# An adaptive-norm block with a long convolution and a shifted MLP on one core: second stage of one transform in groups of three, separate room for one modulation vector, and a new hand-written order

## The chip, the cores and the metric

The kernel runs on one core of one Trainium2 chip. The metric is the device time in microseconds, the median of several executions. Traces come from the hardware profiler and describe one execution each; the clock they name is the TensorE clock that the chip granted, as a share of full speed.

## What is computed

The sequence has S=2048 positions of D=640 channels, and the MLP is F=1728 wide. All inputs are bfloat16. Cut to what matters:

```python
def reference(A_q, A_k, A_v, A_shift_k, A_ssm_k, A_ssm_D, B_x, B_w1, B_w2, B_w3, B_w4, c, w_mod):
    def A(q, k, v, shift_k, ssm_k, ssm_D):
        k_shift = sum over t of k delayed by 3-t, times shift_k[:, 3-t]      # 4 taps
        kv = k_shift * v
        y = irfft(rfft(kv, 2S) * rfft(ssm_k, 2S))[:S]                        # causal, along S
        return q * (y + kv * ssm_D)
    def B(x, w1, w2, w3, w4):
        h = gelu(layernorm(x) @ w1)
        # four quarters of the channels, shifted along S by +1, -1, +2, -2
        x1 = x + concat(shifted quarters of h) @ w2
        return x1 + gelu(layernorm(x1) @ w3) @ w4
    x = A_q
    sa, ca, ga, sb, cb, gb = split(silu(c) @ w_mod, 6)
    h = layernorm(x) * (1 + ca) + sa
    x = x + ga * A(h, A_k, A_v, A_shift_k, A_ssm_k, A_ssm_D)
    h = layernorm(x) * (1 + cb) + sb
    return x + gb * B(h, B_w1, B_w2, B_w3, B_w4)
```

## The kernel before

**The convolution as matmuls.** The transform of length 4096 is done in two stages of 64. The filter ssm_k (called s) and the product kv pass through the same steps. DVE transposes in 32x32 blocks bring the data into slots (`to_slots`, L395). Stage one multiplies by a small constant matrix F1bd (matmuls L408) and writes its result into T01, whose halves T0 and T1 hold 320 of the 640 channels each. Stage two multiplies by the twiddled matrices Gs, kept in tile RG, one for each of 32 values of k. For s, `stage2` (L416 to L432) takes one k at a time over all channels: four matmuls of 64x320 (L425) and one evacuation of 640 elements per partition into KSX, tile R3. For kv, `stage2_half` (L434 to L452) takes three values of k at a time over one half of the channels: twelve matmuls of 64x160 (L446) and one evacuation of 960 elements into XS, tile R5. Every evacuation of PSUM goes through `evac`, whose work lies on ACT (L208) or on DVE (L210), as the order says. Between the two passes `k_shift` (L472 to L489) forms kv from the transposed k and v.

**Inverse stage one** (`inverse1`, L622 to L649) runs ten steps i=0 to 9, five for each half. A step needs KSX also with its two partition halves swapped. Two DMAs make that copy into one of four ring buffers KSY (in RG, RK, RK and Rb), one issued by SP and one by POOL:

```python
for o in range(2):
    dma("SP" if o == 0 else "POOL", 256, lambda q, o=o: q.dma_start(ky[64 * o:64 * o + 64, :], kx[64 - 64 * o:128 - 64 * o, :]), r=[kxk], w=[kk + ("y",)], rate=222.0)
```

DVE then forms two products TA and TB (L632), PE sums them with two constant matrices (L643, L644), and two evacuations write back into T01. **Inverse stage two** (`inverse2`, L664, matmuls L676) reads all of T01 and leaves y for one to three of the 16 sequence tiles at a time. The constants Hs it uses lie in RH, brought there by sixteen small copies at L591.

**The modulation vectors.** `mod_half` (L501 to L527) loads 400 KB of w_mod for half a vector (L503), multiplies by silu(c) (L509) and copies the result into modv. Halves 0 to 5 (sa, ca, ga) come early. Halves 6 to 11 (cb, sb, gb) have their weights in R3, columns 0 to 9600, which KSX occupies until the products have read it.

**Layer norms and the MLP.** ln1, for the first norm, has its statistics on DVE or ACT and a small end (`ln1_fin`, L572 to L577) on POOL. `make_q` (L616, L617) applies sa, ca, ga. `chain_a`, `chain_b` and `chain_c` (L747 to L804) form x after A, then h, then the normed h, with squares summed on ACT at L744 and the small end of the norm at L711 to L734; the first transposes go through PE, later ones through DMA (L780). `mm_w1` (L833, L843, gelu L835 and L849), `mm_w2` (L888, L895), `mm_w3` (L922, gelu L926) and `mm_w4` (L952, L943) follow, and L975 to L984 finish a tile: times gb, plus x, and store. `last_tile` (L986) does that in halves for the last. w1 and w2 go into RG (L1007 to L1010). w3 goes into T0 in one transfer and w4 into T1 in one large and two small ones (L1022 to L1025), once `inverse2` has read T01. x is loaded by `x_load` (L540) twice: into Ra for tiles 0 to 7, and later for tiles 8 to 15 in four pieces of 160 KB for each group of four tiles, called cg0 to cg3.

**What sets the order.** Every step is a task with a number, its engine, its costs and the pieces of tiles that it reads and writes. The string ORDER lists all tasks in the order in which they are issued, with a letter for the engine and the places in PSUM. SP, POOL, DVE, ACT and PE each work through their own part of it strictly in order, and wait where data demand it. So an instruction that waits holds everything behind it on its engine, and a transfer issued by POOL waits for POOL's arithmetic ahead of it.

Of the kernel before, what the change touches and what calls it, by code (L numbers as in the profile page):

```python
# [12 lines left out]
ALU = mybir.AluOpType  # L13
PSUM = bass.MemoryType.PSUM

S, D, F = 2048, 640, 1728
P = 128
NT = S // P
ND = D // P
NF = (F + P - 1) // P  # L20
# [6 lines left out]
18D 19G 20D 50G 21G 23D 22D 25A 27G 29D 30A 36G 37G 24A 28D 31A 2S 0S 68G 4S 26G 69D 90P:0 91A 6S 84P:1 85A 3S 72G 86P:2 87A 5S 32D 73D 102P:3 38G  # L27
104P:0 103A 8S 70G 71D 39G 40A 106P:1 107A 49G 41G 98P:2 88P:3 89A 99A 105D 118P:0 9S 74D 94P:1 75D 95A 112P:3 110P:2 119D 52D 1S 66D 67D 10S 108P:0
111A 113A 109A 42G 11S 43G 44A 33G 116P:1 117D 45D 114P:2 82P:3 54A 96P:0 122P:1 34G 47S 46G 51D 97A 7S 115A 53A 92P:0 35S 201S 48S 12S 93A 83D 76P:3
77A 100P:2 123D 14S 203S 204S 78P:1 101D 80P:0 202S 56G 136D 13S 120P:3 219S 79A 81A 179P:2 55G 180A 193P:1 194A 15S 16S 121D 195P:0 196D 199P:2  # L30
145P:3 200A 147P:1 146D 57G 148A 185P:0 175P:2 176A 186D 141P:3 142D 58G 139P:1 140A 17S 216S 165P:0 166A 177P:2 178D 163P:3 164A 149P:1 150D 59G
189P:0 190A 167P:2 168D 187P:3 188A 143P:1 144D 161P:0 162A 171P:2 172A 181P:3 182D 169P:1 157P:0 65G 158D 170A 159P:2 160A 151P:3 152D 155P:1 153P:0
156A 154D 191P:2 192A 183P:3 184D 173P:1 174A 137P:0 138A 258P:2 250D 197P:3 198A 259A 207D 256P:1 257A 60A 208D 126P:0 127D 264P:3 265A 210A 124P:2
125D 260P:1 261A 61G 251D 62G 266P:3 267A 130P:0 131D 63G 64A 222S 128P:2 129D 252D 205A 220P:1 221A 206D 209G 268P:3 269A 228S 262P:0 263A 272P:1
254P:2 255A 338S 132P:3 133D 134P:0 135D 253D 273A 211A 278P:2 279A 284P:1 270P:3 339G 217P:0 437D 225S 274P:2 285A 223P:1 218A 224D 231S 282P:0 283D
271A 275A 288P:3 289A 280P:1 281D 286P:2 443D 287A 290P:0 229P:3 248S 245G 230D 291A 292P:1 362S 293A 440D 294P:2 295D 304P:3 226P:0 227D 244G 305A
298P:1 306P:2 308P:0 299A 232P:3 446D 309A 276P:1 277A 249G 247S 307D 233D 444D 300P:2 310P:0 311A 246G 301D 312P:3 313D 296P:1 297A 336P:2 337A
302P:0 303D 314P:3 315A 239S 332P:1 333A 238S 237G 328P:2 234G 334P:0 335A 329A 441D 326P:3 327A 341D 322P:1 330P:0 331A 243S 242S 235G 340D 342P:2
343A 344P:3 345A 323D 320P:1 321A 316P:0 317A 241S 240G 236S 346S 348D 347G 349D 350P:2 351A 352P:3 318P:1 319A 356D 354S 355G 357D 358P:0 359A 363G
360P:2 361A 324P:1 325A 370S 364D 365D 368P:0 366P:2 371G 353A 372D 378S 373D 379G 369A 381D 380D 376P:1 374P:3 388D 367A 375A 387G 377A 384P:0 385A  # L40
382P:2 383A 386S 395G 389D 392P:3 390P:1 212G 394S 397D 396D 213A 400P:0 402S 391A 404D 403G 405D 401A 398P:2 399A 393A 421S 422P:1 406P:0 412D 407A
410S 411G 413D 408P:2 418S 445D 416P:3 414P:0 415A 409D 417D 419P:2 420D 436G 442D 452P:30 447D 214A 423D 427S 428P:2 453A 438D 429A 454D 424S 425P:1
426A 430S 431P:3 449A 432A 439D 448D 503D 504D 505A 489P:02 544D 524D 545D 215G 433S 450D 434P:1 537A 525D 435A 547D 456S 526A 527D 455S 546A 557A
490A 467S 506G 507G 482P:31 508D 509D 510A 538D 528G 548G 464S 484A 485G 549D 529D 483A 495P:01 550D 551A 451D 497A 486P:31 530D 531A 469S 511G 512G
462S 496A 491A 487A 463S 532D 533G 552D 553G 459S 461G 466S 572D 573D 574A 465S 575D 576D 577A 488A 513D 514P:0 534D 535P:2 458S 554D 555P:3 515D
521P:0 522A 578D 579G 584A 536D 556D 473D 580D 468S 460S 581D 542P:2 543A 582D 583A 492P:31 494A 540P:0 585D 586D 587A 562P:2 457S 563A 539D 588D
560P:1 519P:2 516D 517D 638D 639D 541A 589G 561A 590A 518D 635D 593D 594P:0 591P:1 520A 564P:2 636D 640A 474D 595D 592D 604P:0 498S 641G 637A 493A
565D 566A 605A 642G 643D 647D 502G 602P:1 603A 567D 568G 475G 648D 558D 649D 650A 569D 570P:3 644D 645D 646A 606P:2 500S 609P:0 571D 620P:1 651D 652G
624P:3 470D 655D 477A 656S 471A 653D 654S 621A 559D 622P:1 657A 625A 665P:3 610D 703D 607D 608A 479D 476D 472G 599D 663P:0 611A 612D 613G 626P:2 704D
623A 666A 614D 615P:1 664A 627A 617D 480A 618P:3 619D 616A 600D 601D 769D 658D 670P:0 671D 667P:2 668D 672A 770D 687P:3 688A 669A 681P:1 596D 501S  # L50
682A 673D 674G 675D 678A 499S 685P:0 676P:2 679P:3 705A 597D 598D 706D 707D 771A 677D 709G 686A 628P:1 629D 708A 683P:2 680A 753P:0 684A 749P:3 710G
715D 747P:1 716D 659D 772D 773D 754A 481G 774A 775D 478G 750A 689P:20 751P:3 794D 711D 712D 713D 776G 690P 777A 714A 717D 781A 782D 719G 718A 748A
720G 721A 722S 783D 784A 778D 791D 779D 780A 785D 786G 789A 630D 631S 723D 724S 725A 733P:1 660D 734A 691D 731P:2 790S 795D 661D 787D 788S 797P:1 634S
732A 735P:2 798A 697D 698D 662D 835D 799P:0 836D 692D 726D 727D 838D 695S 839D 752A 837A 840A 694S 800A 841G 842G 736D 738P:1 739D 741D 755P:32 801P:1
756P 843D 737A 740A 742G 844D 804P:0 743A 792D 845D 846A 847D 848D 849D 744S 850A 802D 803A 745D 702S 746S 819P:1 796D 728D 763D 813P:2 814A 633S 757D
632S 729D 851G 852G 815P:3 853D 730D 895D 854S 820A 855D 856S 859P:2 805D 806A 857P:0 817P:1 896D 793D 860A 758D 761S 807D 700S 808G 811D 809D 693S
858A 861P:2 862D 696S 897A 760S 764D 863A 812S 810S 898D 899D 879P:0 880A 955D 864P:2 900A 865D 818A 866A 767S 875P:0 873P:2 901G 816A 874A 877P:1
821P:32 956D 867D 868G 878A 876A 881P:10 869D 870S 871A 872S 822P 823D 902G 903A 904D 905D 958G 957A 959G 960A 961D 962D 963A 906A 964D 965G 907D 908D
909D 701S 699S 824D 827S 883D 939P:3 940A 910A 933P:1 882P 934A 966D 765S 967S 970P:3 971A 762S 937P:1 938A 911D 912G 915D 913D 914S 916S 919P:3 829D
920A 917P:2 968P:1 826S 918A 768S 969A 921P:3 922D 923A 828S 924P:2 973P:1 523G 925D 766S 884D 935P:3 974D 926A 759S 830D 972G 1007P:2 1008D 976P:1  # L60
977D 927G 979D 832S 1046D 936A 941P:32 943D 1010D 928G 931A 932S 831S 929A 930S 991P:1 885S 975A 889D 825S 890D 891S 978A 980G 942P 886S 987P:3 893S
988A 1009A 888S 989P:0 990A 985P:3 986A 949D 992A 1011G 981D 982S 983D 984S 1020P:2 1021A 1016P:0 1017A 1018P:3 1014P:1 1015A 834S 1019A 993P:20 833S
944D 948S 894S 1012D 1013S 1042P:1 1038P:3 887S 950D 951S 1047D 994P 946S 1043A 953S 995D 1036P:2 954S 1001D 947S 945S 1002D 1022P:10 892S 996D 1000S
997S 952S 1039A 1005S 1006S 1003S 1040P:3 1024D 1004S 1023P 999S 1025D 1028S 1030D 1041A 1027S 1029S 1026S 998S 1031D 1032S 1035S 1033S 1037A 1044P:13
1048D 1049D 1045P 1050S 1053S 1051S 1052S 1054D 1055D 1057A 1058S 1056S 1059A 1034S
# [72 lines left out]
def kernel(  # L138
# [277 lines left out]
    def stage2(XSd, dreg):  # L416
        for k in range(32):
            ps = Slot()

            def f(e, ps=ps, k=k):  # L420
                psv = pst(ps, name="ps_s2")[:, :, 0:320].rearrange("p g (h s) -> p g h s", h=2)
                for cc in range(2):
                    for g in range(2):
                        p = slice(64 * g, 64 * g + 64)
                        nc.tensor.matmul(psv[:, g], lhsT=Gs[p, k, 64 - 64 * cc:192 - 64 * cc], rhs=T1b[p, cc * 32 + k],  # L425
                                         start=(cc == 0), stop=(cc == 1), tile_position=(64 * g, 0))
            t0 = add("PE", 0.275, f, r=[("T01", 0, 20480), ("RG", 192 * k, 192 * k + 192)], alloc=ps, ni=8)
            w = [(dreg, 0, 20480, "s2")]
            if dreg == "R5":
                w += [("kT", 0, 5, "s2"), ("vT", 0, 5, "s2"), ("kTp", 0, 1, "s2")]  # L430
            t1 = evac(XSd[:, :, k, :], lambda t: t[:, :, 0:320].rearrange("p g x -> p x g"), 640, ps, w)
            dep(t1, t0)  # L432

    def stage2_half(h):  # L434
        for k0 in range(0, 32, 3):
            kn = min(3, 32 - k0)
            ps = Slot()

            def f(e, ps=ps, k0=k0, kn=kn, hh=h + 2):
# [159 lines left out]
    for h in range(2):  # L599
        stage2_half(h)  # L600
# [490 lines left out]
```

## Time and profile before

| | |
|---|---|
| runs | 314.98, 316.16, 315.33 us |
| median | 315.33 us |
| profiled execution | 314.98 us, of which the span of the profile is 313.0 us |
| PE, DVE, ACT, POOL busy | 270.4, 219.6, 208.5, 114.2 us |
| DMA moved | 35.75 MB |
| largest groups | L922 64.5 us, L952 59.2 us on PE |

A share of the whole span is a mean over stages that have different limits. The view of slices shows which engine is full at what time; the view of windows gives the busy time of each engine in a stretch; the view of waits says which instruction waited for what; and the chain that ended last follows the end of the kernel back from releaser to releaser. A row of the timeline gives the start, the length, the engine, the line and the tiles (`out<-in`) of one or several like instructions, and in brackets how long the engine stood idle before it and for whom.

### The profile page before, as it was taken

How to read it: one execution, taken by the hardware profiler on the slowest of the kernel's cores; microseconds unless marked ns; L12 is line 12 of the kernel's file. 1: busy time of each engine (PE TensorE's matmuls, PEld its weight loads, DVE VectorE, ACT ScalarE, POOL GpSimd, SP SyncE). 2: the span in 40 equal slices, each digit the busy share in tenths (PEclk: the TensorE clock that was granted, in tenths of full speed). 3: DMA queues.
4: the chain of work that ended last, by engine and by line, in shares of the span. 5: the costliest groups of instructions: out<-in, count | busy, mean ns of one | idle time of the engine just before them, and what ended most of it. 6: DMA issues, size and time to landing. Idle time of an engine off the chain costs nothing.

```text
span 313.0 us, 7669 instructions
## 1 busy us (share of the span) xinstructions
PE 270.4 (86%) x3050; PEld 206.3 (66%) x3054; DVE 219.6 (70%) x446; ACT 208.5 (67%) x351; POOL 114.2 (36%) x240
## 2 busy tenths in 40 slices
PE   0998999999973846687999978989999999999993
PEld 0655655787863624566788756678867887887771
DVE  8998999999964999989776586881627144511332
ACT  4888999999991789998974666625763445252110
POOL 4959333252663377255217520411423132010000
PEclk9999999999995965999999999999999999999998
DMA  6998999988999910521800031043021403131021
GB/s 187 260 220 163 225 205 223 232 217 212 225 276 269 211 37 3 197 100 26 282 24 0 2 68 38 8 94 70 5 54 32 76 0 65 42 70 37 2 71 42
DMA packets 58179, 35.75 MB, mean 114 GB/s; under 512 B 39936, under 2 KB 54912, under 8 KB 58144
## 3 DMA queue, kind: packets, MB, share of 16 engines
q1 hardware_dynamic: 56848, 31.49, 43.2%
q0 software_dynamic: 1200, 3.74, 5.1%
q8 instruction: 24, 0.39, 0.5%
q14 instruction: 11, 0.09, 0.1%
q10 hardware_dynamic: 96, 0.04, 0.1%
HBM read 16.31 MB, written 2.62 MB: 60 GB/s over the span
## 4 chain that ended last, share of the span: by engine, by line
PE 41%; DVE 12%; ACT 6%; DMA 5%; POOL 4%; issue 3%; SPq 0%; ACTq 0%; DVEq 0%; POOLq 0%
PE ps_w L952 15%; PE ps_w L922 14%; PE ps_w L888 5%; PE ps_w L833 3%; ACT RG L744 3%; DMA RG<-R 2%; DVE R L771 2%; DMA R<-RH 1%; DVE Ra L755 1%; POOL lnv L730 1%; PE ps_w1x L843 1%; PE ps_w L943 1%; DVE R L770 1%; PE ps_i L644 1%; DMA R<-RK 1%
## 5 line engine op out<-in xcount | busy, mean ns | idle before, releaser
L922 PE MATMUL ps_w<-R,T 128*128 128x256 bf16 (+1 forms) x630 | 64.5, 261 | 2.3 <-DVE RK L609 1.0
L922 PEld LDWEIGHTS <-T 128*128 128x128 bf16 x630 | 55.6, 98 | 10.2 <-issue 4.0
L926 ACT ACTIVATE R<-ps_w 128x1024 bf16<-128x1024 f32 (+2 forms) x36 | 29.3, 828 | 46.7 <-PE ps_w L922 46.7
L952 PE MATMUL ps_w<-T,R 128*128 128x320 bf16 x416 | 59.2, 299 | 0.0
L952 PEld LDWEIGHTS <-R 128*128 128x128 bf16 x416 | 40.3, 98 | 15.6 <-issue 0.5
L208 ACT CAST T<-ps_s 128x1024 bf16<-128x1024 f32 x35 | 33.3, 1027 | 4.1 <-PE ps_s L408 4.1
L975 DVE TENSOR_TENSOR T<-ps_w,R 128x640 bf16<-128x640 f32 x15 | 12.2, 821 | 29.0 <-PE ps_w L943 18.3
L408 PE MATMUL ps_s<-F1bd,Rb 128*128 128x256 bf16 x160 | 23.0, 294 | 9.4 <-DVE Rb L395 8.6
L744 ACT ACTIVATE RG<-R 128x640 bf16<-128x640 bf16 x32 | 23.4, 733 | 9.0 <-DVE R L895 6.4
L208 ACT CAST R<-ps_s 128x640 bf16<-128x640 f32 (+1 forms) x35 | 26.6, 843 | 0.8 <-PE ps_s L425 0.7
L408 PEld LDWEIGHTS <-Rb 128*128 128x128 bf16 x160 | 16.5, 105 | 15.4 <-DVE Rb L395 8.8
L644 PE MATMUL ps_i<-EB,Rb 128*128 128x128 bf16 x160 | 20.3, 227 | 6.7 <-DVE Rb L632 6.7
L895 DVE SCALAR_TENSOR_TENSOR R<-ps_w,R 128x640 bf16<-128x640 f32 x16 | 13.1, 821 | 18.5 <-PE ps_w L888 17.9
L730 POOL TENSOR_TENSOR lnv<-lnv,mhalf 128x2 f32<-128x2 f32 (+1 forms) x29 | 23.1, 796 | 2.3
L888 PE MATMUL ps_w<-RG,R 128*128 128x320 bf16 x160 | 23.6, 299 | 0.0
L208 ACT CAST T<-ps_i 128x1024 bf16<-128x1024 f32 x18 | 17.6, 1126 | 8.9 <-PE ps_i L644 8.9
L729 POOL TENSOR_TENSOR lnv<-stat,lnv 128x2 f32<-128x2 f32 x19 | 5.8, 306 | 46.0 <-ACT RG L744 31.6
L833 PE MATMUL ps_w<-R,RG 128*128 128x256 bf16 (+1 forms) x200 | 19.0, 251 | 3.2 <-ACT Rb L208 1.4
L643 PE MATMUL ps_i<-EA,Rb 128*128 128x128 bf16 x160 | 20.5, 227 | 1.4 <-DVE Rb L632 1.1
L644 PEld LDWEIGHTS <-Rb 128*128 128x128 bf16 x160 | 16.3, 103 | 7.4 <-DVE Rb L632 7.4
L833 PEld LDWEIGHTS <-RG 128*128 128x128 bf16 x200 | 16.4, 98 | 5.1 <-issue 2.4
L888 PEld LDWEIGHTS <-R 128*128 128x128 bf16 x160 | 15.4, 98 | 5.9 <-issue 0.3
(178 smaller groups left out, 528.5 us busy)
## 6 DMA issues: line engine op xcount, KB each, us to landing
Ra<-in_A_ssm_k_dram SPq DMA_DIRECT2D x5, 512.0 KB, 6.0
R<-in_w_mod_dram SPq DMA_DIRECT2D x6, 400.0 KB, 8.4
out_dram<-RH SPq DMA_DIRECT2D x60, 40.0 KB, 1.6
T<-in_B_w_dram SPq DMA_DIRECT2D x1, 2160.0 KB, 8.9
T<-in_B_w_dram SPq DMA_DIRECT2D x1, 2080.0 KB, 9.4
RH<-in_w_mod_dram SPq DMA_DIRECT2D x4, 400.0 KB, 4.6
Ra<-in_A_q_dram SPq DMA_DIRECT2D x4, 320.0 KB, 5.2
RK<-R POOLq DMA_DIRECT2D x5, 256.0 KB, 6.5
```

What stands on the lines that cost most here:

```text
L208: nc.scalar.copy(dst, src(ps.tile))
L408: nc.tensor.matmul(psv[:, ml, :], lhsT=xL[:, s0:s0 + P], rhs=F1r, start=True, stop=True)
L643: nc.tensor.matmul(psv[:, w, :], lhsT=Av[:, r_, :, g_], rhs=EAf, start=True, stop=False)
L644: nc.tensor.matmul(psv[:, w, :], lhsT=Bv[:, r_, :, g_], rhs=EBf, start=False, stop=True)
L730: nc.gpsimd.tensor_tensor(rs, rs, mhalf[:, 0:n], ALU.pow)
L744: add("ACT", 0.74, lambda e: nc.scalar.activation(junk, src, ACT.Square, scale=float(D) ** -0.5, accum_out=stat[:, li, 1, t:t + 1]), r=[sk ...
L833: nc.tensor.matmul(pt[:, fb, 0:cw], lhsT=w1_sb[:, b, 160 * fb:160 * fb + P], rhs=hT[:, b, 0:cw], start=(b == 0), stop=(b == ND - 1))
L888: nc.tensor.matmul(pt[:, hf, 0:320], lhsT=gsf[:, fb, c0:c0 + P], rhs=w2_sb[:, fb, 320 * hf:320 * hf + 320], start=(fb == 0), stop=(fb == 4))
L895: t1 = add("DVE", 0.82, lambda e, ps=ps, hv=hv, ix=ix: nc.vector.scalar_tensor_tensor(hv, ps.tile[:, :, 0:320], 1.0, hv, ALU.mult, ALU.add ...
L922: nc.tensor.matmul(pt[:, fl, 0:cw], lhsT=w3_sb[:, b, fb * P:(fb + 1) * P], rhs=xT[:, b, 0:cw], start=(b == 0), stop=(b == ND - 1))
L926: nc.scalar.activation(g3[g % 2][:, f0:f0 + fn, 0:cw], ps.tile[:, 0:fn, 0:cw], ACT.Gelu_apprx_tanh)
L952: nc.tensor.matmul(bank(i, hf), lhsT=gg[:, fb, i * P:(i + 1) * P], rhs=w4_sb[:, fb, 320 * hf:320 * hf + 320], start=(fb == 0 and i == 0), ...
```

## The change

Second stage of s: `stage2` is gone, and s goes through `stage2_half` as kv does, half by half. Of 32 evacuations of 640 elements 22 remain, twenty of 960 and two of 640; of 128 matmuls 64x320 there are 256 of 64x160. A group of the first half needs only the first half of T01.

Weights of modulation halves 10 and 11 (gb) go to R5, columns 13824 to 17024, in place of R3; the readers of cb and sb now depend on halves 6 to 9 alone.

w3 is loaded in five transfers of 128 rows and the main part of w4 in three, beside the two small ones as before.

The order is new throughout. What it moves:

- On POOL, `ln1_fin` of tiles 4 to 6 stands ahead of all the copies of `inverse1` but the first, and there is no arithmetic of POOL between copies i=1 and i=9.
- The copies of Gs (L354, L355) are all on SP, where three were on POOL. Two groups of angle operations (L307) go from POOL to DVE, and one at L349 from DVE to POOL.
- SP issues all loads of s before any transpose of k and v, the loads of x(0:8) earlier, and modulation halves 0 to 5 after all transposes.
- SP's queue at the end of `inverse1` is: half 7, copies i=8 and i=9, halves 9, 6, 11, 8, a piece of w2, half 10, w1, then pieces of x(8:16) among pieces of w2, then w3 in five with three of the pieces of x or w2 among them, w4's first small piece, x, two transposes, w4's second small piece and w4 in three (rows 8 to 13 first).
- `inverse2` takes its tiles in other groups: 0 to 2, then 14 and 15 with 3 and 4, 8 to 10, 5 to 7, and so on, and tiles 11 to 13 last, behind the w1 matmuls of the first tiles.

```diff
-    def stage2(XSd, dreg):
-        for k in range(32):
...
-                        nc.tensor.matmul(psv[:, g], lhsT=Gs[p, k, 64 - 64 * cc:192 - 64 * cc], rhs=T1b[p, cc * 32 + k],
-                                         start=(cc == 0), stop=(cc == 1), tile_position=(64 * g, 0))
...
-            t1 = evac(XSd[:, :, k, :], lambda t: t[:, :, 0:320].rearrange("p g x -> p x g"), 640, ps, w)
-    def stage2_half(h):
+    def stage2_half(XSd, dreg, h):
         for k0 in range(0, 32, 3):
             kn = min(3, 32 - k0)
...
-            w = [("R5", 10240 * h, 10240 * h + 10240, "s2"), ("kT", 4 * h, 5, "s2")] + ([("vT", 0, 5, "s2")] if h else [("kTp", 0, 1, "s2")])
-            t1 = evac(XS[:, 160 * h:160 * h + 160, k0:k0 + kn, :],
+            w = [(dreg, 10240 * h, 10240 * h + 10240, "s2")]
+            if dreg == "R5":
+                w += [("kT", 4 * h, 5, "s2")] + ([("vT", 0, 5, "s2")] if h else [("kTp", 0, 1, "s2")])
+            t1 = evac(XSd[:, 160 * h:160 * h + 160, k0:k0 + kn, :],
                       lambda t, kn=kn: t[:, :, 0:480].rearrange("p g (k s) -> p s k g", k=3)[:, :, 0:kn], 320 * kn, ps, w)
...
-    stage2(KSX, "R3")
+    for h in range(2):
+        stage2_half(KSX, "R3", h)
...
-    wl = [(R3[:, o:o + 1600].rearrange("p (b n) -> p b n", b=ND), ("R3", o, o + 1600)) for o in range(0, 9600, 1600)]
+    wl = [(R3[:, o:o + 1600].rearrange("p (b n) -> p b n", b=ND), ("R3", o, o + 1600)) for o in range(0, 6400, 1600)]
+    wl += [(R5[:, o:o + 1600].rearrange("p (b n) -> p b n", b=ND), ("R5", o, o + 1600)) for o in (13824, 15424)]
...
-    dma("SP", 2200, w3t[0], w=[("T01", 0, ND * FP)])
-    dma("SP", 2200, w3t[1], w=[("T01", 10240, 10240 + NF * D, "w4")])
+    for b in range(ND):
+        dma("SP", 440, lambda q, b=b: q.dma_start(w3_sb[:, b, 0:F], B_w3[b * P:(b + 1) * P, :]), w=[("T01", b * FP, b * FP + FP)])
+    for f0, f1 in ((0, 4), (4, 8), (8, NF - 1)):
+        dma("SP", 165 * (f1 - f0), lambda q, f0=f0, f1=f1: q.dma_start(w4_sb[:, f0:f1, :], B_w4[f0 * P:f1 * P, :].rearrange("(b p) n -> p b n", p=P)),
+            w=[("T01", 10240 + D * f0, 10240 + D * f1, "w4")])
```

## The prediction

> **What bounds the kernel now.** I first read the slices, to see which engines are full at which time, and then asked for the busy time of every engine stage by stage. The columns are the window, its length, the busy time of PE, PEld, DVE, ACT and POOL with their instructions, the granted clock, the DMA share and GB/s.
>
> ```profile
> 70.00:91.20 21.20, 19.10 (x351) 17.18 (x346) 20.93 (x20) 21.17 (x27) 12.28 (x16) 1.00 1.00 225
> 91.20:97.80 6.60, 1.65 (x23) 1.24 (x20) 0.03 (x1) 3.11 (x4) 0.08 (x1) 0.80 1.13 266
> 97.80:104.20 6.40, 5.11 (x65) 5.08 (x66) 5.77 (x6) 1.01 (x1) 2.60 (x4) 0.67 1.10 310
> 112.00:126.00 14.00, 7.15 (x239) 4.83 (x232) 13.57 (x38) 13.26 (x26) 10.87 (x27) 0.51 0.01 4
> 126.00:144.80 18.80, 13.85 (x234) 10.93 (x233) 17.32 (x50) 17.48 (x41) 7.83 (x20) 1.00 0.35 124
> 144.80:313.00 168.20, 157.54 (x1380) 123.84 (x1377) 88.74 (x222) 83.91 (x157) 39.00 (x105) 0.99 0.22 52
> ```
>
> There are three regimes. From 6 to 91 us (the convolution) PE, DVE and ACT are all nearly full. From 105 to 144.8 us (layer norms, w1, w2) DVE and ACT are the limit, 13.6 and 13.3 of 14 us in the fourth row. From the first w3 matmul at 144.79 us PE is the limit: 157.5 of 168.2 us. Between the first two lies a hole: 91.2 to 97.8 us, DVE idle, and after it 6.4 us at a clock of 0.67.
>
> Next the waits, the chain that ended last and the POOL and SP timelines, to see who made the hole:
>
> ```profile
> DVE Rb L632 <- DMA RG<-R: 6.6, 1, 6.6
> ```
> ```profile
> 90.12 7.49 DMA RG<-R
> ```
> ```profile
> 80.94 0.51 POOL L628 DMA_DIRECT2D Rb<-R  x1 [1.76 <-DVE Rb L632]
> 81.47 1.50 POOL L572 TENSOR_TENSOR nb<-mv 128x1 f32<-128x1 f32 x1
> ...
> 89.10 1.09 POOL L577 TENSOR_SCALAR nb<-nb 128x2 f32<-128x2 f32 x1
> 90.12 0.62 POOL L628 DMA_DIRECT2D RG<-R  x1
> ```
> ```profile
> 82.95 0.46 SPq L628 DMA_DIRECT2D RG<-R  x1
> ```
>
> The ninth product of inverse1 (i=8, TB) needs a half-swapped copy of KSX, one half issued by SP and one by POOL (L628). SP issued its half at 82.95. POOL stood in ln1_fin (L572 to L577) from 81.47 to 90.19 and issued 7.2 us later; the landing took 7.49 us. That 6.6 us wait is one of the few on the path.
>
> Last, the third regime's data: w3 is one transfer held at the head of SP until the last inverse2 matmul has read T0.
>
> ```profile
> SPq L1022 <- PE ps_i L676: 17.4, 1, 17.4
> ```
> ```profile
> T<-in_B_w_dram SPq DMA_DIRECT2D x1, 2160.0 KB, 8.9
> ```
>
> Issued at 127.30, landed at 136.2, used at 144.79: 8.6 us to spare.
>
> **Stage two of s.** Removed: 32 evacuations of 640 (ACT 0.645 us start to start, from 19 in 12.26; DVE 0.773, from 13 in 10.05) and 128 matmuls of 64x320 (112 in 9.80 us, 87 ns each, paced by the evacuations). Added: 20 evacuations of 960 and two of 640 (ACT 0.82, from 9 in 7.38; DVE 1.09) and 256 matmuls of 64x160 (68 in 2.71 us, 40 ns). The two evacuators together did 1/0.645 + 1/0.773 = 2.84 per us, so 32 took 11.3 us; now 20 at 1/0.82 + 1/1.09 = 2.13 per us take 9.4, and two more 0.7: 10.1 us. PE: 256 x 40 ns = 10.2 us against some 9 to 11. So PE and evacuators are now matched; the gain is at most 1.2 us, and a loss of 1 us if the extra 128 matmuls lie uncovered. I count it with the whole stage below, at about 1.
>
> **The order of the copies.** ln1_fin of tiles 4 to 6 moves on POOL ahead of the copies i=1 to 9. The 8.7 us then delay no copy; the copies wait only for their ring buffers. What is late next? The products themselves: DVE's row of work. Up to its last L632 product DVE has 85.4 us of work before and 85.9 after (counted task by task with durations from these rows: seven fewer evacuations of ACT's, some statistics and angles more on DVE). It starts at 6.2 us and lost some 3 us to small gaps before 91 us. So its last product ends at 6.2 + 85.9 + 3 = 95, where it now ends at 101.4. ACT's count goes from 84.5 to 82.2 us, and the ten last evacuations still follow the products. The slow clock goes with the idle time: the inverse1 matmuls took 0.11 us apart until 102.2 and 0.06 after, 40 of them, 2 us. Inverse1's last evacuation falls from 105.2 to about 98, gain 7. Ends: gain 8 if the extra gap time also goes, 5 if a smaller hole stays. For that speaks bandwidth: a pair of copies moves 512 KB, and a pair per 2.3 us (two products of 1.14 us) is 220 GB/s, the 225 of the first window, so copies can't run ahead much; and copies 1 and 2 now wait behind mod 5 and sixteen L591 copies in the queues (SP's took 6.3 us there): 0 to 1.5 us.
>
> The four Gs copies on SP, k and v transposes behind the s loads, mods 0 to 5 later: SP issues them before 35 us, where DVE transposes at 1.9 to 2.1 us each set the pace; I price them at 0, and between 2 us gained (SP stood 2.3 us at the angles' result in the Gs copies) and 1 us lost. The two angle operations moved POOL to DVE are in the count.
>
> **Last modulation vector.** Its two 400 KB weights go to R5 and must wait for the products i=6 to 8 that read XS there. The vector is needed only at the first w4 output (L980, 180.7 us), a cover of some 70 us: nothing. But the wait stands on SP, and behind it queue mod 8, w1, w2 and x(8:16). The product i=8 should end at 92 to 93, so SP issues mod 8 at 93, and it lands 8.4 us later (the median of the six), at 101 to 102. The first who needs it is L771 of chain_b, 9.3 us after inverse1's end before (114.47), so at 107: 5 us of cover, nothing; if it were gone, each us late would be a us on the path. w1 and x were issued from 92.1 on, their first use came at 124.7 (L843); a few us later on SP and 7 earlier in use leave some 20.
>
> **The layer-norm stage.** Same arithmetic in another order: DVE 37.3 before and 35.5 after, ACT 38 and 37. It took 39.6 us before (105.2 to 144.79). I take 38.5, bounds 36.5 and 41. First w3 matmul at 98 + 38.5 = 136.5.
>
> **w3 and w4.** The new order puts the last inverse2 behind the first tiles' w1: about 26 us after inverse1 instead of 22, so 124.5. Behind it on SP come five w3 pieces and, between them, two loads of x and a w2 piece of 280 KB together. Moved at the 240 GB/s of the one transfer (2160 KB in 8.9 us), 2.45 MB take 10 us: landing at 134.7 to 137. The 8.6 us of cover are gone, and the first w3 matmul is due at 136.5. The first piece lands earlier, but every output tile needs all five. I price it 0.5, bounds 0 and 4. The x loads behind w3 (cg3, cg0) feed ln1 statistics due 1 to 3 us after the first w3 matmul; landing at 137 to 138 they cost 0 to 1. w4 in three is asked for 13.8 us after the first w3 matmul and is on SP behind two transposes; it lands at some 13: 0 to 1.5, taken as 0.5.
>
> The Trainium skill, page "DMA: Bandwidth & Descriptors", section "Bandwidth", measurements, says to batch transfers to 1 MiB or more for 75% of peak; its section "Anatomy of one DMA" fits 2.0 us plus bytes over 436 GB/s for each, so five pieces of 440 KB one after the other would be an estimated 15 us against 7 for one, and w3 would land near 140, 3.5 us late. No run here shows pieces of w3.
>
> Against that stands the trace's own row: six modulation loads of 400 KB, issued in a row, moved while the chip drew 266 to 310 GB/s, more than the single 2160 KB transfer's 240. Pieces in flight overlap; so I add nothing.
>
> **From the first w3 matmul on** the same tasks remain in both (36 w3, 17 w4, 12 w1, 13 w2). PE 157.5 busy, 5 us tail, 5.7 us idle before; the largest idles were 1.75 and 0.98 us at 184 to 190 for a transposed tile, which came late because POOL's ln1_fin lay in front. I take 5.5 + 5 + 0.5 + 0.5 of idle: 169, bounds 165 and 174.
>
> **Sum.** 136.5 + 169 = 305.5 span. The profiled execution had a span of 313.0 and a time of 314.98, so 2.0 lies outside it and it is 0.35 under the median of 315.33: 307.5, and on the median's scale 307.9; I say 308.
>
> **Rivals.** *The cover of w3 is gone, moderate:* the hole goes, but 2 to 4 us come back as w3, x and w4 land late, or the layer norms stretch to 41: 310 to 313. For it: the 8.6 us shrink to none by my own sum. Against: the transfers have the queue to themselves (4 GB/s drawn at 112 to 126).
>
> *Slower: w3 becomes what PE waits for.* Place: SP's L1022 wait. If the last inverse2 slips from 124.5 to 135 or beyond (its evacuation and L676 work compete with layer norms on full DVE and ACT), w3 lands at 135 + 10 = 145, later than now, and x's cg3 and cg0 quarters behind it. The 8 us of gain are all spent then, and w4 behind w3 adds 1 to 3: 316.5 to 319. It decides from a last inverse2 at about 136. Against: inverse2 needs only inverse1 (98), and its last 96 matmuls take 1.2 us.
>
> *The hole moves:* POOL no longer delays the copies, but copies and mods share the DMA engines (share 1.13, landings 6 to 7.5 us for 256 KB), so DVE waits 1 to 2 us at several products: inverse1 ends at 103 to 104, and the total is 313.8 to 316: no change.
>
> **How the numbers follow.** Forecast (305 to 310): 0.50. Cover gone (310 to 313.7): 0.22. Hole moves: 0.10. Slower by w3: 0.18. A change of 0.5% is about what a measurement of this kernel can tell from none: 313.75 to 316.9. Faster 0.72, same 0.10, slower 0.18. The range: low 303.5 takes the upper gain in the convolution and a layer-norm stage of 36.5; high 316 takes in the cases with cover gone and the moved hole, leaving most of the slower one out.
>
> **What would show it.** Right: POOL issues each L628 within 1 us of SP; no L632 wait over 2 us; last L632 near 95; no clock of 0.67 at inverse1's end; first L922 at 135 to 138. The PE stretch after it at 167 to 171. Wrong: an L922 wait on DMA of over 4 us, a last L676 later than 130, DVE idle before L632 adding to more than 5 us, or the layer norms over 41 us.

## The result, and the profile after

The changed kernel takes 302.24 us (median of 4 runs, 300.44 to 303.35) where the kernel before takes 315.75 us (median of 4 runs, 314.98 to 318.61): a ratio of 0.955, interval 0.947 to 0.963. It is faster by 13.5 us. The prediction was 308.0 with a range of 303.5 to 316.0; the time lies 1.3 us below the range. In later comparisons, which had 7 to 19 runs of the kernel before each, that kernel's median was 316.6 to 317.7 us.

The profiled execution took 300.44 us, the shortest of the four, with a span of 298.7. First the stages, from the view of windows (length; busy time of PE, PEld, DVE, ACT and POOL with their instructions; granted clock; DMA share; GB/s):

```profile
70.00:91.00 21.00, 18.89 (x340) 17.30 (x340) 20.87 (x21) 20.95 (x27) 3.57 (x7) 1.00 0.98 240
91.00:96.80 5.80, 5.32 (x78) 4.59 (x76) 5.77 (x12) 5.80 (x8) 4.45 (x5) 1.00 0.98 287
96.80:104.00 7.20, 4.97 (x234) 3.25 (x234) 7.06 (x17) 5.52 (x12) 3.89 (x8) 0.91 1.08 285
104.00:116.00 12.00, 9.45 (x242) 6.61 (x242) 11.47 (x32) 10.65 (x23) 8.00 (x24) 0.63 0.24 52
116.00:135.70 19.70, 14.05 (x218) 10.72 (x216) 16.62 (x46) 17.83 (x41) 8.19 (x25) 0.91 0.43 135
135.70:298.70 163.00, 156.55 (x1380) 124.17 (x1378) 89.96 (x217) 87.18 (x163) 38.61 (x108) 1.00 0.23 53
```

The hole is gone: where DVE had 0.03 of 6.6 us it now has 5.77 of 5.8, right up to inverse1's end at 96.8, and the clock there is 1.00. The layer norms still keep DVE and ACT nearly full. The last row is shorter by 5.2 us with the same 1380 PE instructions.

On POOL's timeline the last copies of inverse1 follow each other at DVE's pace, 2.27 us apart, each released by a product, and `ln1_fin` (L557 to L562 here) is done at 56.2 us, 7 us before the second of POOL's copies:

```profile
55.96 0.27 POOL L562 TENSOR_SCALAR nb<-nb 128x2 f32<-128x2 f32 x1
...
80.46 0.51 POOL L613 DMA_DIRECT2D Rb<-R  x1 [1.76 <-DVE Rb L617]
82.73 0.51 POOL L613 DMA_DIRECT2D RG<-R  x1 [1.76 <-DVE Rb L617]
85.00 0.51 POOL L613 DMA_DIRECT2D RK<-R  x1 [1.76 <-DVE Rb L617]
```

What ended the idle time of PE in the last stretch, by the view of waits: ahead the six waits of the kernel before, from 144.8 us on, which sum to 5.6 us, and then the three of the changed kernel, from 135.7 us on, which sum to 1.8.

```profile
PE ps_w1x L843 <- DMA R<-RK: 1.7, 1, 1.7
PE ps_w L922 <- DVE RK L609: 1.0, 1, 1.0
PE ps_w L833 <- DMA R<-RK: 1.0, 1, 1.0
PE ps_w1x L843 <- ACT RG L744: 0.7, 1, 0.7
PE ps_w L922 <- ACT R L926: 0.7, 1, 0.7
PE ps_w L922 <- DMA R<-RH: 0.5, 1, 0.5
```
```profile
PE ps_w L907 <- DMA R<-RH: 0.7, 1, 0.7
PE ps_w L818 <- DMA R<-RK: 0.6, 1, 0.6
PE ps_tr L772 <- DVE RH L724: 0.5, 1, 0.5
```

No wait of PE on w3 or w4 is among them. SP's wait for the last `inverse2`, and the landings of w3's five pieces and of w4's three:

```profile
SPq L1012 <- PE ps_i L661: 16.0, 1, 16.0
```
```profile
L1012 SPq DMA_DIRECT2D T<-in_B_w_dram x5: 352/432/584, 122.2 to 125.1; - x5
...
DMA to landing us min/median/max: 3.3/6.2/7.9
```
```profile
L1014 SPq DMA_DIRECT2D T<-in_B_w_dram x3: 506/515/583, 139.5 to 140.7; - x3
...
DMA to landing us min/median/max: 6.3/7.4/8.5
```

The last w3 piece was issued at 125.1 and landed at most 7.9 us later, by 133.0; the first w3 matmul ran at 135.74. w4 landed by 149.2; its first matmul ran at 149.60. Both arrive in time, w4 by a hair.

So the 14.3 us between the two profiled spans are 8.4 before inverse1's end (105.2 to 96.8), 0.7 in the layer norms (39.6 to 38.9) and 5.2 after the first w3 matmul (168.2 to 163.0). Of the 5.2, 3.8 are PE waits, 1.0 is PE's busy time (157.54 to 156.55) and 0.3 is the tail after the last matmul. A word on the code: `inverse2` works on the same groups of tiles in both kernels; it is their sequence that is new.

### The profile page after: what moved, and what is told of

Read it like the earlier page. It is cut to its first block, busy times and chain, and to the rows that moved or that the text cites. A ratio compares the mean times of both kernels' runs of the same rounds, so it can differ in the third digit from the quotient of the medians.

```text
span 298.7 us, 7890 instructions
## 1 busy us (share of the span) xinstructions
PE 269.7 (90%) x3176; PEld 208.5 (70%) x3182; DVE 218.2 (73%) x438; ACT 208.3 (70%) x341; POOL 104.8 (35%) x237
## 4 chain that ended last, share of the span: by engine, by line
PE 51%; DVE 13%; ACT 11%; DMA 10%; POOL 6%; issue 5%; SPq 2%; DVEq 0%; POOLq 0%; ACTq 0%
PE ps_w L937 17%; PE ps_w L907 14%; ACT T L207 5%; DMA Ra<-in_A_q_dram 5%; PE ps_w L873 4%; PE ps_w L818 3%; PE ps_s L427 3%; ACT RG L729 3%; DVE Rb L617 3%; PE ps_ksh L463 2%; POOL lnv L715 2%; PE ps_s L407 2%; DMA RK<-R 2%; DVE R L756 2%; PE ps_mod L493 2%
## 5 line engine op out<-in xcount | busy, mean ns | idle before, releaser
L907 PE MATMUL ps_w<-R,T 128*128 128x256 bf16 (+1 forms) x630 | 63.8, 261 | 0.7 <-DMA R<-RH 0.7
L207 ACT CAST T<-ps_s 128x1024 bf16<-128x1024 f32 x32 | 30.4, 1029 | 3.2 <-PE ps_s L407 3.1
L207 ACT CAST R<-ps_s 128x960 bf16<-128x960 f32 (+1 forms) x35 | 30.8, 964 | 1.8 <-PE ps_s L427 1.6
L407 PEld LDWEIGHTS <-Rb 128*128 128x128 bf16 x160 | 16.7, 107 | 14.7 <-DVE Rb L394 8.6
L427 PE MATMUL ps_s<-T,RG 64*128 64x160 bf16 x512 | 21.2, 230 | 0.8 <-ACT R L207 0.6
L427 PEld LDWEIGHTS <-RG 64*128 64x128 bf16 x512 | 17.7, 94 | 5.1 <-issue 4.6
L818 PE MATMUL ps_w<-R,RG 128*128 128x256 bf16 (+1 forms) x200 | 20.0, 259 | 1.3 <-DMA R<-RK 0.6
L629 PE MATMUL ps_i<-EB,Rb 128*128 128x128 bf16 x160 | 19.0, 219 | 1.5 <-DVE Rb L617 1.4
L628 PE MATMUL ps_i<-EA,Rb 128*128 128x128 bf16 x160 | 19.0, 219 | 0.4 <-ACT R L207 0.3
L714 POOL TENSOR_TENSOR lnv<-stat,lnv 128x2 f32<-128x2 f32 x19 | 4.0, 212 | 40.9 <-ACT RG L729 28.7
```

Of the source, the lines that this page charges most:

```text
L207: nc.scalar.copy(dst, src(ps.tile))
L407: nc.tensor.matmul(psv[:, ml, :], lhsT=xL[:, s0:s0 + P], rhs=F1r, start=True, stop=True)
L427: nc.tensor.matmul(psv[:, g, j], lhsT=Gs[p, k, 64 - 64 * cc:192 - 64 * cc], rhs=T1h[h][p, cc * 32 + k], start=(cc == 0), stop=(cc == 1), t ...
L628: nc.tensor.matmul(psv[:, w, :], lhsT=Av[:, r_, :, g_], rhs=EAf, start=True, stop=False)
L629: nc.tensor.matmul(psv[:, w, :], lhsT=Bv[:, r_, :, g_], rhs=EBf, start=False, stop=True)
L818: nc.tensor.matmul(pt[:, fb, 0:cw], lhsT=w1_sb[:, b, 160 * fb:160 * fb + P], rhs=hT[:, b, 0:cw], start=(b == 0), stop=(b == ND - 1))
```

## The experiments

The theory after the result: one POOL task made the hole, and the hole's end plus the order behind the first w3 matmul make the gain; threes, pieces and room for gb bring little by themselves. The rivals: the threes shorten the convolution; the pieces of w3 and w4 let work start earlier; the last stretch is short only because more was done before it. Names with b_ are the kernel before with an edit, names with a_ the changed kernel with one. The column us is the median of the runs; the ratio is to the kernel before in the same comparison. The stages are those of the one profiled execution of each: the first `inverse2` matmul, from there to the first w3 matmul, and from there to the end of the span.

| kernel | us | ratio to before (interval) | inverse1 ends | layer norms | from first w3 |
|---|---|---|---|---|---|
| before | 315.75 | | 105.3 | 39.5 | 168.2 |
| changed | 302.24 | 0.955 (0.947 to 0.963) | 96.9 | 38.8 | 163.0 |
| b_fin_late | 311.19 | 0.982 (0.974 to 0.989) | 97.9 | 41.7 | 168.4 |
| a_fin_back | 307.98 | 0.970 (0.963 to 0.976) | 103.6 | 39.0 | 162.9 |
| b_threes | 319.96 | 1.009 (1.005 to 1.013) | 111.8 | 39.5 | 167.9 |
| b_threes2 | 317.35 | 1.002 (0.999 to 1.006) | 109.2 | 39.5 | 168.2 |
| b_tail | 314.84 | 0.992 (0.988 to 0.996) | 107.3 | 39.8 | 166.2 |
| a_tail | 312.15 | 0.987 (0.982 to 0.992) | 97.9 | 39.8 | 173.0 |
| b_tailfins | 316.76 | 0.998 (0.994 to 1.002) | 108.4 | 39.6 | 167.8 |
| b_feeds_apart | 321.58 | 1.012 (1.005 to 1.020) | - | - | - |
| a_w_one | 303.54 | 0.958 (0.953 to 0.964) | 97.8 | 39.2 | 162.8 |
| b_fin_gb | 309.48 | 0.975 (0.969 to 0.980) | 98.5 | 40.0 | 168.6 |
| b_fin_gb_tail | 306.20 | 0.966 (0.959 to 0.973) | 97.5 | 40.0 | 166.0 |
| b_fin_gb_tail2 | 307.11 | 0.967 (0.963 to 0.971) | 98.1 | 41.7 | 165.4 |
| a_out_act | 301.87 | 0.951 (0.946 to 0.957) | 98.3 | 39.7 | 163.3 |

The profiled execution of b_feeds_apart, 323.26 us, was the longest of its six, so its stages are not set beside the others.

### The hole by itself: b_fin_late and a_fin_back

```diff
 POOL's part of ORDER, kernel before (b_fin_late)
  copy i=7
- ln1_fin(4..6)
  copy i=8
  copy i=9
+ ln1_fin(4..6)
 POOL's part of ORDER, changed kernel (a_fin_back)
- ln1_fin(4..6)
  copies i=1 .. i=7
+ ln1_fin(4..6)
  copy i=8
```

> The kernel before with one task moved: POOL's ln1_fin of tiles 4 to 6 goes behind the last copy of inverse1 (i=9) instead of between i=7 and i=8; nothing else changes. Theory (the hole is POOL's order alone): no wait of L632 on a copy over 2 us, inverse1's last evacuation at 98 to 99 instead of 105.2, the rest shifted unchanged, so a ratio of 0.977 to 0.982 (about 308.5 us). Rival (the hole comes from bandwidth, or the threes of stage two are what shortens the convolution): DVE still idles 3 us or more before products 8 or 9, inverse1 ends at 102 or later, ratio 0.99 to 1.0.

> The changed kernel with that ln1_fin put back on POOL between the copies i=7 and i=8. Theory: the copy i=8 is issued some 8 us late, DVE idles 5 to 7 us, inverse1 ends at 103 to 105 instead of 96.8, and the run takes 308 to 310 us. Rival (the copies in the new order have slack, because all are issued earlier): DVE idles less than 2 us and the time stays within 303 us.

With one task moved, the kernel before ends inverse1 at 97.9 us, as expected, and no product waits 2 us for a copy. Put back, the task makes the hole again in the changed kernel: the view of waits and POOL's timeline, both of a_fin_back, have it.

```profile
DVE Rb L617 <- DMA RG<-R: 4.1, 1, 4.1
```
```profile
81.77 0.51 POOL L613 DMA_DIRECT2D Rb<-R  x1 [1.76 <-DVE Rb L617]
82.30 0.45 POOL L557 TENSOR_TENSOR nb<-mv 128x1 f32<-128x1 f32 x1
...
88.42 0.64 POOL L613 DMA_DIRECT2D RG<-R  x1
```

The wait was 4.1 us, less than the 5 to 7 expected. The task took 6.1 us here and 8.7 in the kernel before, and it is not quite the same task: six instructions here and eight there, since its first two run once for each tile whose statistics come from ACT, one tile here and two there. The time, 307.98, is at the low end of what was expected. So the hole is POOL's order, shown from both sides. The ratio of b_fin_late, 0.982, is at the edge of the expected 0.977 to 0.982; the time, 311.2, is above the 308.5 named with it, in part because the kernel before had 316.6 in this comparison. But the layer norms took 41.7 us, 2.2 longer. ACT's timeline in it shows who stood:

```profile
107.63 0.42 ACT L524 CAST modv<-ps_mod 128x320 bf16<-128x320 f32 x1 [2.94 <-PE ps_mod L509]
```

That is the evacuation (the copy out of PSUM) of the last half of gb. ACT comes to it 7 us earlier than before, and behind it in ACT's order stand the squares (L744) of the first layer norms. What it waited for was PE:

```profile
104.72 1.43 PE L676 MATMUL ps_i<-T,RH 32*32 32x160 bf16 x74 [3.17 <-issue]
106.08 1.51 PE L509 MATMUL ps_mod<-R,silu_w 128*128 128x320 bf16 x5
```

PE ran the five matmuls of that half at 106.08, behind a part of `inverse2` ahead of which it had stood 3.17 us, for a reason that the profile does not show ("issue"). gb's weights were not late: the last of the six loads that bring halves 6 to 11 was issued at 92.5, and each landed within 7.6 us, so all by 100.1.

```profile
L503 SPq DMA_DIRECT2D R<-in_w_mod_dram x6: 681/1160/1968, 83.8 to 92.5; - x6
...
DMA to landing us min/median/max: 4.4/6.5/7.6
```

### Room for gb: b_fin_gb

```diff
 beside b_fin_late
- readers of cb, sb: ("modB", 6, 12), gb's weights in R3
+ readers of cb, sb: ("modB", 6, 10), gb's weights in R5 at 13824
- PE half 11, ACT half 11: ahead of chain_b
+ behind the first ends of chain_b (44 and 42 places later)
```

> The kernel before with ln1_fin of tiles 4 to 6 behind the last copy, and with gb taken out of the layer norms' way as the changed kernel does it: its weights in R5, chain_b no longer depends on it, and the matmuls and the evacuation of half 11 stand 44 and 42 places later in the order, behind chain_b's first ends. In the run with the moved ln1_fin alone ACT stood 2.9 us at that evacuation (it waited for weights that came no earlier than before), and the layer-norm stage took 41.7 us instead of 39.6. Theory (gb's weights took that back): the stage is 38.5 to 40 us, the time 308 to 310 us (2 us under the run with the moved ln1_fin alone, 311.2). Rival (the stage is longer because the x and w1 transfers are late): it stays at 41 to 42 us, time 311.

The wait of ACT is gone, the layer norms take 40.0 us, and the time is 309.48, 1.7 us under b_fin_late. The stage agrees with the theory, but its reason, late weights, does not hold, as the loads of b_fin_late show: PE has such a gap here too (2.67 us ahead of the same part of `inverse2`), and ACT no longer has an instruction that waits for it there. The edit gives gb its room, frees the readers of cb and sb and moves the half at once; which of the three is needed is not shown. The two intervals of the times overlap, so the wait and the stage carry this, not the times alone.

### Threes alone: b_threes and b_threes2

```diff
 kernel before
- stage2(KSX, "R3")
+ for h in range(2):
+     stage2_half(KSX, "R3", h)
 ORDER: 22 of the 32 places of the old pairs; b_threes in the order k=0, 3, ..
 b_threes2: in the changed kernel's order, four PSUM places in rotation
```

> The kernel before with the second stage of s alone in threes of one half (256 matmuls 64x160, 22 evacuations, 12 of them on ACT and 10 on DVE or near that), in the places in the order where the 32 of one k stood. Theory: the stage is 1 us shorter at most and the hole after it stays, so a ratio of 0.995 to 1.003. Rival (threes carry the convolution's gain): inverse1's last product ends 3 us or more earlier, ratio under 0.99.

> Again the kernel before with the second stage of s alone in threes, now with the groups in the sequence of the changed kernel (which starts at k=27 to 31 and so does not wait for the first half of Gs) and with the four PSUM places in rotation. The first form had PE waits of 4.8 us in this stage, for a Gs copy and for evacuations. Theory (the threes themselves cost and bring within 1 us): stage two ends within 1 us of the 40.5 us of the kernel before, ratio 0.996 to 1.004. Rival (threes in this place are slower, since two evacuators take 960 at 0.82 and 1.09 us and nothing lies between): PE waits of 3 us or more on evacuations remain, ratio over 1.007.

The first form lost 5 us in this stage: the first product of inverse1 starts at 75.7 us and not at 70.4. PE's timeline in it, columns as ever, shows that the place in the order made this and not the threes: it waits first for a Gs copy, since groups starting at k=0 need the half of Gs that comes later, and then for PSUM.

```profile
31.99 1.55 PE L427 MATMUL ps_s<-T,RG 64*128 64x160 bf16 x39 [1.00 <-DMA RG<-RG]
34.61 1.84 PE L427 MATMUL ps_s<-T,RG 64*128 64x160 bf16 x48 [1.07 <-DVE R L209]
38.58 1.42 PE L427 MATMUL ps_s<-T,RG 64*128 64x160 bf16 x36 [1.05 <-DVE R L209]
```

With the changed kernel's sequence of groups (b_threes2) the products start at 71.3 us, where the kernel before and the variants that keep its first stages have 70.4 to 71.1, and the time is the same: 1.002, interval 0.999 to 1.006. The threes by themselves bring nothing.

### Pieces of w3 and w4: a_w_one

```diff
 changed kernel
- for b in range(ND): dma("SP", 440, ... w3_sb[:, b, 0:F] ...)
+ dma("SP", 2200, w3t[0], ...)
- for f0, f1 in ((0, 4), (4, 8), (8, NF - 1)): dma(... w4_sb[:, f0:f1, :] ...)
+ dma("SP", 2200, w3t[1], ...)
```

> The changed kernel with w3 in one transfer, issued where its first piece was, and the main part of w4 in one, where its first piece was. Theory (pieces are worth nothing: w3 lands 3 us before its use either way, w4 about when it is used): first w3 matmul within 1 us of 135.7, time within 1 us of the changed kernel's 302.2, 0 to 0.7 us lost at the first w4 matmul. Rival by the price of a transfer (pieces cost 2 us each): one transfer lands 2 to 8 us earlier and the time falls by up to 1 us. Rival the other way (pieces let work start early): the first w3 or w4 matmul waits 2 us or more on the transfer.

The first w3 matmul is at 137.0, 39.2 us after inverse1's end, the rest takes 162.8 us, and the ratio of 0.958 lies inside the changed kernel's interval. The first w3 matmul and the time are both 1.3 us later than in the changed kernel, a little outside the 1 us expected; 0.9 us of it had come before inverse1's end, ahead of either transfer. PE waits for neither w3 nor w4, and neither rival shows. The Trainium skill, page "DMA: Bandwidth & Descriptors", section "Anatomy of one DMA", gives for a transfer that GpSimd issues a fit of 2.0 us plus the bytes over 436 GB/s, by which five pieces of 440 KB one after the other would take an estimated 15 us. Here SP issued them, and all five, with 0.28 MB of other loads between them, were in within 10.8 us of the first issue (122.2 to 133.0); pieces and whole arrive in time alike.

### The order behind the first w3 matmul: b_tail, a_tail, b_fin_gb_tail, b_fin_gb_tail2

```diff
 b_tail: ORDER = before's tasks that the changed kernel issues ahead of its first w3 matmul,
                 in before's sequence; then the rest in the changed kernel's sequence
 a_tail: the same the other way round
 b_fin_gb_tail: b_tail on b_fin_gb
 b_fin_gb_tail2: and on DVE, at the seam
- norms (L610, wait for POOL), two additions of w2's output (L896)
+ additions, norms
```

> The kernel before up to its first w3 matmul, and from there on the order of the changed kernel (with w4 in one transfer, as before). The hole stays. Theory (what comes after the first w3 matmul got faster by its order, 5.2 us in the two profiles): the first w3 matmul stays at 144 to 146 us, the stretch from there to the end falls from 168.2 to 163 or 164 us, ratio 0.984 to 0.988. Rival (the stretch got faster because what it waits for was done earlier, relative to the first w3 matmul): it stays at 166 to 169 us, ratio 0.995 to 1.003.

> The changed kernel up to its first w3 matmul, and from there on the order of the kernel before (w3 and w4 in pieces all the same). Theory (the order behind the first w3 matmul is worth some 5 us of its own): inverse1 and the first w3 matmul stay at 97 and 136 us, the stretch from there to the end grows from 163.0 to 167 to 169 us, with the waits of L828 and L818 on a transposed tile back, and the time is 305 to 308 us. Rival (the stretch is short because of what the earlier stages leave behind): it stays at 163 to 165 us, time under 304.

> The same, and from the first w3 matmul on the order of the changed kernel. So it holds the hole, gb and the later order, and lacks the threes of stage two, the pieces of w3 and w4 and the new order of everything else before inverse1. Theory (these three carry the gain): inverse1 ends at 97 to 99, first w3 matmul at 136 to 138.5, the rest 163 to 166.2 us (the upper end holds the seam of some 2 us that the graft cost the kernel before), time 302 to 306 us, ratio 0.957 to 0.967. Rival (the new order of the first stages carries 3 us or more beyond the hole): 307 us or more.

> The kernel before with ln1_fin moved, gb out of the way and the later order of the changed kernel, as in the run before, and now without the seam: two DVE additions of w2's output (L896), which stood behind two norms that wait for POOL and kept PE for 1.84 us at the third and fourth w3 group, go ahead of these norms. Theory (the later order alone brings the whole difference of the stretch after the first w3 matmul): the two waits go, the stretch falls from 166.0 to 164 us or less, near the changed kernel's 163.0, time 303.5 to 305 us. Rival (the later order brings half, the rest comes from what the first stages leave behind): the waits come back elsewhere, stretch 165.5 us or more, time 306.

No theory's number came out for the stretch of b_tail and a_tail: b_tail took 2.0 of the 5.2 us, with 166.2 just inside its rival's range, and a_tail overshot by 4 to 6. The seam explains much of it. A graft joins two orders whose engines are not at the same point, and its first 7 to 9 us hold longer waits than either parent has there. PE's timeline of a_tail:

```profile
141.93 1.28 PE L907 MATMUL ps_w<-R,T 128*128 128x128 bf16 x20 [1.87 <-ACT R L911]
146.26 1.23 PE L828 MATMUL ps_w1x<-R,RG 128*128 128x256 bf16 x5 [3.06 <-DMA R<-RK]
147.28 3.92 PE L818 MATMUL ps_w<-R,RG 128*128 128x256 bf16 x20
```

The seam can be left out by counting from the first w1 group of the stretch (L843, or L828) to the end of the span. The kernel before needs 313.0 - 149.89 = 163.1 us from there, the changed one 298.7 - 140.88 = 157.8. With the changed order grafted on, the kernel before needs 159.0 (b_tail), 158.7 (b_fin_gb_tail) and 158.4 (b_fin_gb_tail2); with the old order grafted on, the changed kernel needs 164.4 (a_tail), or about 162.3 without 2.1 us of slow matmuls right at the seam (5 and 20 matmuls took 1.23 and 3.92 us in place of the 0.71 and 2.35 of the undisturbed kernels). Of the 5.3 us between the parents, 1.2 are work that the changed order has put ahead of that point (ten small w3 matmuls and ten transposes, in the grafts as well); of the other 4.1 the grafts have 2.9 to 3.5. So most of it is the order alone, whatever stood ahead of it; 0.6 to 1.2 us are not accounted for. Whether the waits at the seam gave the other engines a lead that shortens what follows is not shown; a_tail, which has the longest of them, gains at most 0.8 us on the order it took over (162.3 against 163.1).

b_fin_gb_tail, with the hole, gb and the later order together, has 0.966 where the changed kernel has 0.955, and its 306.2 us lie just above the expected 302 to 306. In the profiles it is 4.8 us longer: 0.6 up to inverse1's end, 1.2 in the layer norms and 3.0 behind them, of which 1.8 are waits at the seam.

b_fin_gb_tail2 did not do what it should: the two waits of 0.82 and 1.02 us went, one of 2.17 us for a transposed tile took their place, and stretch and time (165.4 and 307.1 us) came near the rival's 165.5 and 306.

```profile
146.24 0.73 PE L788 MATMUL ps_tr<-RG,RH 128*128 128x128 bf16 x10 [2.17 <-DVE RH L740]
```

### Which steps of the later order: b_tailfins and b_feeds_apart

```diff
 kernel before, POOL (b_tailfins)
+ ln1_fin(14, 15), ln1_fin(12, 13)
  end of chain_a, tiles 7 and 8
- ln1_fin(14, 15), ln1_fin(12, 13)
  end of chain_a, tiles 9 and 10
 kernel before, DVE, ACT, POOL and PE (b_feeds_apart)
- chain_b of tiles 9, 10 between the steps of tiles 7, 8; w1 of 9, 10 right behind w1 of 7, 8
+ chain_b of tiles 9, 10 behind tiles 7, 8; w1 of 9, 10 behind two w2 blocks and a w4 block
```

> The kernel before with two POOL tasks moved: ln1_fin of tiles 14, 15 and of 12, 13, which stood at 166.6 to 173 us ahead of the layer norm's end of tiles 9 and 10 (chain_a), now stand ahead of chain_a's end of tiles 7 and 8. Theory (these 6.4 us of POOL make the feed of w1 late at 185 to 190): the PE waits of 1.75 and 0.98 us on a transposed tile go, the stretch after the first w3 matmul falls from 168.2 to 165 to 166.5 us, ratio 0.989 to 0.995. Rival (it is the place of the w4 matmuls and their DVE work that makes the feed late): the waits stay, stretch 167.5 to 169, ratio 0.997 to 1.004.

> The kernel before with the order changed around 185 to 195 us alone: the twelve steps of chain_b and chain_c for tiles 9 and 10 (w1's sixth feed) stand behind those for tiles 7 and 8 (its fifth) on DVE, ACT and POOL, and PE takes w1 of tiles 9 and 10 not right behind w1 of tiles 7 and 8 but after two w2 blocks and the next w4 block. Theory (before, both feeds are due within 4 us and are made interleaved; the changed order has 13 us between them): the PE waits of 1.75 us (L843) and 0.98 us (L833) go, the stretch after the first w3 matmul falls from 168.2 to 165.3 to 166.7 us, ratio 0.990 to 0.996. Rival (DVE is the limit there, whatever the sequence): the waits appear at the next w2 or w4 block instead, stretch 167.5 or more.

b_tailfins changed one of the two waits from 1.75 to 0.84 us and left the other; the stretch fell by 0.4 us and the time is the same. b_feeds_apart (321.58 us, ratio 1.012, interval 1.005 to 1.020) did remove both waits: the fifth feed's w1 followed the w4 block at once. But PE's timeline of its profiled execution shows longer ones behind it:

```profile
191.20 2.88 PE L888 MATMUL ps_w<-RG,R 128*128 128x320 bf16 x20 [2.05 <-ACT R L835]
...
211.42 4.00 PE L922 MATMUL ps_w<-R,T 128*128 128x256 bf16 x18 [3.27 <-DVE R L752]
```

The first is w2 behind a gelu (L835) that ACT reaches late; the second is w3, and the profile puts it down to a step of `chain_a` on DVE (L752). The rival was nearer. No single step of the later order has been found that carries its 3 us; which steps do it together stays open.

### Stores of the last tile: a_out_act

```diff
-                qe = ("SP", "ACT")[cg % 2] if hf else "SP"
+                qe = ("SP", "ACT")[cg % 2]
```

> The changed kernel with two of the last tile's first four stores issued by ACT instead of SP. In its profile SP issued the last two stores up to 296.44, 1.57 us after their data was ready at 294.87, because two stores of the first half and one of another tile were ahead; ACT was idle. Theory: SP ends 0.5 to 0.9 us earlier, the span from the last matmul to the end falls from 4.7 to about 4.1 us, time 0.4 to 0.7 us lower, under what a comparison of times can resolve. Rival (the landing of the stores sets the end, not their issue): 4.7 us stay.

From the end of the last matmul to the end of the span it is 4.2 us (297.1 to 301.3), against 4.7 in the changed kernel (294.0 to 298.7). The mechanism holds. The time, 301.87 against 302.24, is as low as the changed kernel's, and no comparison here separates the two.

## Why the prediction was right and wrong

**What bounds the kernel** was read rightly: the three regimes and the hole, which one POOL task made.

**Convolution, 7 us put, bounds 5 to 8; measured 8.4 in the profiled pair, 9 over the runs.** The mechanism was right, the size too small. Two terms: the last product ended at 93.8, not 95, since DVE worked 85.05 us between 6.2 and 93.8 and not 85.9, and stood idle 2.5 us and not 3; and the hole of the profiled execution was a short one. In the three profiles set in the table that kept the old first stages whole (before, b_tail, b_tailfins) inverse1 ended at 105.3, 107.3 and 108.4, mean 107.0; in four with the hole alone removed (b_fin_late, b_fin_gb and the two grafts on it) at 97.9, 98.5, 97.5 and 98.1, mean 98.0. The wait of DVE in b_tailfins was

```profile
DVE Rb L632 <- DMA RG<-R: 8.3, 1, 8.3
```

where the profiled execution had 6.6. A sum made on one execution took that execution's hole for the usual one.

**Threes of stage two, 1 us put: 0** (b_threes2). Everything in this stage that gained was the copies. Four runs of the changed first stages (the changed kernel, a_tail, a_w_one, a_out_act) end inverse1 at 97.7 on the mean, 0.3 us from the 98.0 of the moved task alone.

**The last modulation vector, priced at nothing: right in the sum, wrong in the reason.** The sum for the layer norms was 38.5 us, measured 38.9. But it was taken for free because gb is needed late. The prediction did not see that in the old order half 11's evacuation stood on ACT ahead of the layer norms and would wait 2.9 us there for PE as soon as the hole was gone. Moving it out of the way took back 1.7 us of stage (b_fin_late 41.7, b_fin_gb 40.0); the other 1.2 us down to the changed kernel's 38.8 are the rest of the new order, not taken apart.

**w3's cover, priced 0.5, bounds 0 to 4: 0.** The last inverse2 began at 120.5 and SP issued at 122.2, 2.3 us before the 124.5 put; the landing was by 133.0 and not at 134.7 to 137. The cover is 2.7 us, not gone. The 15 us that the prediction estimates by the fit of the Trainium skill's page did not come about; the page gives it for transfers that GpSimd issues, and these are SP's, which the prediction does not say. The rivals *cover gone* and *slower by w3* both fell with that. w4 has 0.4 us to spare, and the x loads behind w3 held nobody up.

**From the first w3 matmul, 169 us put, bounds 165 to 174; measured 163.0. This is the step that failed.** It failed where it said that the same tasks remain and then took over the old order's idle time ("5.5 + 5 + 0.5 + 0.5"). The changed kernel has 1.8 us of PE waits and a tail of 4.7. The grafts show that the order of this stretch, which was not costed at all, is worth about 3 us by itself (2.9 to 3.5). The prediction had named a cause for the two largest idles, POOL's `ln1_fin`; with it moved (b_tailfins) one fell from 1.75 to 0.84 us and the other stayed. All the terms of 0.5 for w3 and w4 were zero as well. Had the low bound of this term been PE's busy time and tail alone, 157.5 + 5 = 162.5, the range would have held the result. The range's low end has a slip besides: 97 + 36.5 + 169 and the 2.35 us up to the median's scale make 304.9, not 303.5.

**The hole moves** did not happen: no product waited 2 us on a copy, with 240 GB/s moved in the first row above. By the prediction's own terms this rival comes to 312.9 to 313.9 us (103 to 104, 38.5, 169 and 2.35), not to 313.8 to 316.

## What to carry to other kernels

A wait of the critical engine for half a transfer is worth asking which queue issued the late half and what stood in front of it: here one arithmetic task on POOL, on columns of one or two elements, cost the convolution 9 us, and moving that task, with what it uncovered, is more than half of the gain (ratio 0.975 of 0.955). When such a stall goes, look for what was late anyway and hidden by it: the evacuation of a vector that nobody needed yet took 2 us back until it was moved too. And a stretch with the same tasks in a new order has a term of its own; take its bounds from the engine's busy time alone up to the old idle time, because moving single steps by hand (two tries here) shortened one wait or made others, and the kernel became no faster.

## What the runs showed of the hardware

A PE wait can be followed by slow matmuls, so that it may cost more than its length. In b_fin_gb_tail2 PE was idle for 2.14 us and then ran at a lower granted clock; the windows of that run (columns as above):

```profile
132.00:135.10 3.10, 0.97 (x9) 0.62 (x8) 2.57 (x9) 3.04 (x8) 1.49 (x3) 1.00 0.00 0
135.10:139.80 4.70, 4.70 (x26) 3.00 (x27) 1.99 (x7) 0.94 (x4) 2.10 (x9) 0.64 0.00 0
```

Its 20 w2 matmuls (L889) took 4.52 us there and 2.88 in b_fin_gb_tail, which had the same wait of 2.14 us ahead of them and no drop of the clock (1.00 from 134.5 to 137.5): 1.6 us in one of two nearly equal kernels, each profiled once. What decides it is not shown. The Trainium skill, page "TensorE: Matmul & The Clock Gate", section "Why this matters for your kernels", puts the idle gap to avoid at over some 3 us; here one of 2.14 us was followed by the drop in one of these two profiles.

POOL's small instructions took very different times for the same work: the six instructions of `ln1_fin` of tiles 4 to 6 lasted 2.2 us (54.00 to 56.23) where the changed kernel has them, and 6.1 us (82.30 to 88.42) between the copies in a_fin_back. Why is not shown.
